# Threshold attention and an MLP mixer on one core: the order of work in the first row, and a weight conversion with one two-operand VectorE step

## The chip, the cores and the metric

The kernel runs on one core of a Trainium2 chip. The metric is the device time of one execution in microseconds (us). Executions of one kernel mostly agree within 0.3%; the state of a run is judged by the clock granted to TensorE and by comparison with the fastest run of the same kernel, and all runs used here are fast ones. Ratios below are the mean time of one kernel's fast runs over that of the other's fast runs of the same rounds, so they are not quite the ratios of the medians that stand beside them.

Engine names in the profile: PE is TensorE (PEld its weight loads), DVE is VectorE, ACT is ScalarE, POOL is GpSimd, SP is SyncE, which here issues DMAs.

## The reference

```python
scores = np.matmul(q, k.transpose(0, 1, 3, 2)) / 8          # q, k, v: 8 x 8 x 576 x 64
thresh = np.max(scores, axis=-1, keepdims=True) - tau
scores = np.where(scores >= thresh, scores, -1e9)
attn = softmax(scores) ; x = heads side by side of attn @ v  # x: 8 x 576 x 512
h   = np.maximum(x^T @ w_tok1, 0) @ w_tok2                   # mixes tokens
u   = x + h^T
out = u + np.maximum(u @ w_ch1, 0) @ w_ch2                   # mixes channels
```

The four weights arrive as 64-bit floats. Before their first use the kernel turns them into 32-bit floats, in 31 pieces, of which 26 have 512 columns.

## The kernel before

The program walks over units: a unit is 128 queries of two heads. For each it makes scores (TensorE), their maxima (VectorE), a bias (GpSimd), a Prelu that applies the threshold and an exponential with sums (ScalarE), and, one unit later, reciprocals (VectorE) and the scaling by them (GpSimd). Two units later the weights of attention are transposed. In the first row (units 0 to 17, batch 0) TensorE does that in three groups of three, each into one PSUM buffer, of which there are two; VectorE or ScalarE then copies the group into SBUF. From the second row on, other code with DMAs does this, and the mixer of the batch before fills TensorE.

```python
def turn(u, third):                     # first row only
    ps = ps_tr.tile([P, MAIN], F32, tag="tr", ...)            # pool of two PSUM buffers
    for c in range(3): nc.tensor.transpose(out=ps[:, c, :], in_=e[...], identity=ident)
    on = nc.scalar.copy if third == 1 and u % 2 else nc.vector.tensor_copy
    on(out=eTs[key][:, 3*third : 3*third+3, ...], in_=ps)

for u in range(...):                    # cut to what the change touches; w = u - 2
    scores(u)                           # TensorE; then maxima on VectorE, bias on GpSimd
    ...                                 # values of earlier units, norm(u - 1)
    if b_now: weight(2)                 # second row: 2 of 6 conversion steps a unit
    else:     weight_to(2.25 * (u - 1.5))
    ...
    for i in range(3): turn(w, i)       # first row
    ...
    if on: weigh(u)                     # Prelus and exponentials, ScalarE
    if b_now: weight(2)
    elif u == 0: ...
    else: weight_to(2.25 * (u - 1))     # the rest of 2.25 steps a unit
```

`weight` runs conversion steps. A piece has three on VectorE, two passes on ScalarE for the piece after it, and an addition on GpSimd, after which the next load into that buffer may start. In the traces VectorE runs its instructions in the order in which the program issues them (in the unit from 43.65 us shown below: maxima, reciprocal, steps, copies). The pool of two buffers decides when the program is built which buffer each group gets; it need not alternate.

Of the kernel before, what the change touches and what calls it, by code (L numbers as in the profile page):

```python
# [9 lines left out]
F32 = mybir.dt.float32  # L10
U32 = mybir.dt.uint32
I32 = mybir.dt.int32
I64 = mybir.dt.int64
AF = mybir.ActivationFunctionType
ALU = mybir.AluOpType
# [6 lines left out]
def kernel(  # L22
# [25 lines left out]
    nc = tc.nc  # L48
# [113 lines left out]



    raws = {}

    def load_piece(i):
# [16 lines left out]
    def wide(i):  # L184
        return i < len(pieces) and pieces[i][1].dtype == I64

    def on_scalar(i, part):
        if wide(i):
            lo, hi, h2 = raws[i]
            if part == 0:  # L190
                nc.scalar.activation(out=lo.bitcast(I32), in_=lo, func=AF.Copy, scale=2.0**-29)
            else:
                nc.scalar.activation(out=h2, in_=hi.bitcast(F32), func=AF.Square)

    def on_vector(i, part):
        if wide(i):
            dst = pieces[i][0]
            lo, hi, h2 = raws[i]
            bits = dst.bitcast(U32)
            if part == 0:  # L200
                nc.vector.tensor_scalar(
                    out=bits, in0=hi, scalar1=3, scalar2=0x3FFFFFFF, op0=ALU.logical_shift_left, op1=ALU.bitwise_and
                )
            elif part == 1:
                nc.vector.scalar_tensor_tensor(  # L205
                    out=bits, in0=hi, scalar=0xC0000000, in1=bits, op0=ALU.bitwise_and, op1=ALU.bitwise_or
                )
            else:
                nc.vector.scalar_tensor_tensor(out=dst, in0=h2, scalar=2.0**-30, in1=dst, op0=ALU.is_ge, op1=ALU.mult)

    def on_gpsimd(i):
        if i >= 0:
# [10 lines left out]
    def weight(n):  # L223

        nonlocal steps_done
        for k in range(steps_done, min(steps_done + n, 3 * len(pieces) + 1)):
            i, part = divmod(k, 3)
            if part == 0:
                on_gpsimd(i - 1)
                if i:  # L230
                    load_piece(i - 1 + NRAW)
            else:
                on_scalar(i + 1, part - 1)
            on_vector(i, part)
            steps_done = k + 1

    def weight_to(x):

        weight(max(int(x) - steps_done, 0))
# [36 lines left out]
    def in_blocks(b):  # L276
        return b > 0
# [10 lines left out]
    def scores(u):  # L288
        b, p0, t = units[u]
        sc = [  # L290
            (ps_3rd if b == 0 and (2 * u + h) % 3 == 2 else ps_sc).tile([P, 2, MAIN], F32, tag="sc", name=f"sc{h}_{u}") for h in range(2)
        ]
        if t == SHARED:
            parts = [(b * NP + p0, slice(MAIN, S), slice(0, 64)), (b * NP + p0 + 1, slice(0, LAST), slice(64, P))]
        else:
            o = P * t if t < SHARED else LAST + P * (t - SHARED - 1)
            parts = [(b * NP + p0 + (t > SHARED), slice(o, o + P), slice(0, P))]
        order = [(f, part, h) for f in range(2) for part in parts for h in range(2)]
        for f, (n, cols, rows), h in order if b else sorted(order, key=lambda o: o[2]):
            r = slice(D * h, D * h + D)  # L300
            qT, kT = heads[n]
            nc.tensor.matmul(sc[h][rows, f, 0:HS], lhsT=qT[r, cols], rhs=kT[r, HS * f : HS * f + HS], start=True, stop=True)  # L302
        mx = small.tile([P, 2], F32, tag="mx", name=f"mx_{u}")
        bias = small.tile([P, 2], F32, tag="bias", name=f"bias_{u}")
        for h in range(2):
            c = slice(h, h + 1)
            nc.vector.tensor_reduce(out=mx[:, c], in_=sc[h][:, :, 0:HS], axis=AX.XY, op=ALU.max)  # L307
            nc.gpsimd.tensor_scalar(out=bias[:, c], in0=mx[:, c], scalar1=toff, scalar2=-SCALE, op0=ALU.add, op1=ALU.mult)  # L308
        st[u] = sc, bias

    def weigh(u):
        sc, bias = st.pop(u)
        rs = small.tile([P, 2], F32, tag="rs", name=f"rs_{u}")
        e = work.tile([P, 2 * S], F32, tag="e", bufs=3, name=f"e_{u}")
        for h in range(2):
            eh = e[:, S * h : S * h + S].rearrange("p (f x) -> p f x", f=2)
            nc.scalar.activation(out=eh, in_=sc[h][:, :, 0:HS], func=AF.Prelu, bias=bias[:, h : h + 1], scale=SCALE, alpha=STEEP)  # L317
        st[u] = e, rs

        if b_now:  # L320
            fill(0.2)
        for h in range(2):
            eh = e[:, S * h : S * h + S]
            nc.scalar.activation(out=eh, in_=eh, func=AF.Exp, bias=ntau, accum_out=rs[:, h : h + 1])  # L324
            if b_now:
                fill(0.2)
# [13 lines left out]
    def turn(u, third):  # L340

        b, p0, t = units[u]
        key, place = (b, p0, t // GU), t % GU
        e = st[u]

        if third == 0 and place == 0:
            eTs[key] = work.tile([P, NK, GU * P], F32, tag="T", name=f"eT_{u}")
        if third == 2:
            st.pop(u)
        ps = ps_tr.tile([P, MAIN], F32, tag="tr", name=f"tr{third}_{u}")[:, 0 : 3 * P].rearrange("p (c x) -> p c x", c=3)  # L350
        for c in range(3):
            k0 = (3 * third + c) * P
            nc.tensor.transpose(out=ps[:, c, :], in_=e[:, k0 : k0 + P], identity=ident)  # L353
        on = nc.scalar.copy if third == 1 and u % 2 else nc.vector.tensor_copy
        on(out=eTs[key][:, 3 * third : 3 * third + 3, P * place : P * place + P], in_=ps)

    def turn_blocks(u):
# [149 lines left out]
    def fill(share):  # L507
        nonlocal credit
        credit += share * quota
        while todo and credit > 0:  # L510
            cost, step = todo.popleft()
            credit -= cost
            step()
        if not todo:
            credit = 0.0
# [18 lines left out]
    b_now = 0  # L534
# [12 lines left out]
    for u in range(len(units) + LAG + 4):  # L547
        on = u < len(units)
        if u == UB:
            late.close()  # L550
            ps_mm = ctx.enter_context(tc.tile_pool(name="ps_mm", bufs=2, space=bass.MemoryType.PSUM))
        if on:
            b_now, p0, t = units[u]
            n = b_now * NP + p0
        w = u - LAG
        back = 0 <= w < len(units)
        if on:
            scores(u)

        last = False  # L560
        if due and not in_blocks(due[0][1]):
            last = values_due(u)
        if 0 < u <= len(units):
            norm(u - 1)
        if b_now:
            weight(2)
        else:

            weight_to(2.25 * (u - 1.5))
        while copies:  # L570
            copies.popleft()()
        if last:
            push(0)
        if back:
            wb, wp, wt = units[w]
            if not in_blocks(wb):
                for i in range(3):
                    turn(w, i)
            if wt % GU == GU - 1:
                g = wt // GU  # L580
                if g < 2:
                    split_middle(wb * NP + wp + g)
                due.append((u + (2 if in_blocks(wb) else 1), wb, wp, g))
        if b_now:
            fill(0.4)
        if back and in_blocks(wb):
            turn_blocks(w)
        if b_now:
            weight(2)
        if on:  # L590
            weigh(u)
        elif b_now:
            fill(0.6)
        if b_now:
            weight(2)
        elif u == 0:
            on_scalar(0, 0)
            on_scalar(0, 1)
        else:
            weight_to(2.25 * (u - 1))  # L600
        if on:


            when = {3: (2, 0, 2), 4: (2, 2, 4), 5: (2, 4, 6), 6: (2, 6, 8), 8: (3, 0, 3), 0: (1, 3, 6), 1: (1, 6, 8)}
            if u == 0:
                load_qk(1, (nc.sync, nc.sync), range(0, 3))
            if t in when:
                m, lo, hi = when[t]
                if n + m < len(pairs):
                    load_qk(n + m, (nc.scalar if b_now else nc.sync,) * 2, range(lo, hi))  # L610
            if t in (3, 7) and n + 2 + t // 4 < len(pairs):
                load_v(n + 2 + t // 4)
            if t == 2:
                prep(n + 1)
            if t == 7 and n + 2 < len(pairs):
                prep(n + 2)
        if due and in_blocks(due[0][1]):
            values_due(u)
# [31 lines left out]
```

## Time and profile before

| | before |
|---|---|
| median, lowest, highest of 3 runs | 1380.67, 1376.87, 1382.66 us |
| span of the profiled run | 1375.1 us |
| TensorE busy | 1322.7 us, 96% |
| VectorE, ScalarE, GpSimd busy | 588.2, 581.8, 356.0 us |

The page's picture of the kernel before, in 40 slices of 34.4 us each (a digit is the busy share in tenths):

```profile
PE   6877799999999999999999999999999999999998
DVE  6788875445444443434244444434333453201000
```

TensorE has room only in the first six slices, about 206 us. From 16 to 206 us VectorE is busy for 156.9 us and TensorE for 155.2; ScalarE (123.3) and GpSimd (110.5) have less to do. The prediction below shows these stages one by one. The profiled run is the fastest of the three (1376.94 us in the record of the profile), so its stages may be shorter than typical; ratios, not two profiles, carry the sizes below.

### The profile page before, as it was taken

What the parts mean: (1) busy time and instruction counts of PE and PEld (TensorE: products, weight loads), DVE (VectorE), ACT (ScalarE), POOL (GpSimd) and SP (SyncE); (2) the same over time, 40 slices, a digit from 0 to 9 for tenths busy, and PEclk for the clock granted to TensorE, in tenths of its full rate; (3) what the DMA queues carried; (4) which work ended last, traced back from release to release, by engine and by line L of the source; (5) the groups of instructions that cost most, each with busy time, mean ns of one, the idle gap of its engine ahead of it and who ended that gap; (6) DMA issues with size and microseconds to landing.
All of it is one profiled execution on the core that took longest, in us unless ns stands there. A gap on an engine that the chain in (4) does not pass through costs nothing.

```text
span 1375.1 us, 17691 instructions
## 1 busy us (share of the span) xinstructions
PE 1322.7 (96%) x6226; PEld 817.9 (59%) x6226; DVE 588.2 (43%) x1017; ACT 581.8 (42%) x1288; POOL 356.0 (26%) x683
## 2 busy tenths in 40 slices
PE   6877799999999999999999999999999999999998
PEld 3444465646565666565665567565656576575675
DVE  6788875445444443434244444434333453201000
ACT  5666654454445444443434444353333444120110
POOL 4555653222222222222122222222121222100000
PEclk9988999999999999999999999999999999999999
DMA  5434655454544354433344435434433442400000
GB/s 121 98 96 125 183 142 124 100 123 98 122 109 114 82 121 94 113 88 95 77 100 94 113 77 123 106 83 98 103 87 75 107 103 63 115 1 16 8 11 21
DMA packets 278871, 128.20 MB, mean 93 GB/s; under 512 B 200896, under 2 KB 271552, under 8 KB 278784
## 3 DMA queue, kind: packets, MB, share of 16 engines
q1 hardware_dynamic: 150176, 111.06, 32.0%
q10 hardware_dynamic: 128608, 16.01, 7.3%
q8 instruction: 50, 0.82, 0.3%
q14 instruction: 37, 0.30, 0.1%
HBM read 43.25 MB, written 9.44 MB: 38 GB/s over the span
## 4 chain that ended last, share of the span: by engine, by line
PE 85%; DVE 7%; DMA 2%; SPq 2%; ACT 1%; issue 1%; POOL 1%; ACTq 0%; DVEq 0%; POOLq 0%
PE c L486 26%; PE c L470 26%; PE sc L302 11%; PE pv L413 9%; PE t L441 5%; PE t L448 3%; PE pv L408 3%; DVE mx L307 2%; SPq L374 2%; PE tx L432 1%; PE c L482 1%; DMA eT<-T 1%; PE tr L353 1%; DVE wc L205 1%; ACT e L317 1%
## 5 line engine op out<-in xcount | busy, mean ns | idle before, releaser
L307 DVE TENSOR_REDUCE mx<-sc 128x1 f32<-128x576 f32 x288 | 204.5, 751 | 487.9 <-PE sc L302 487.5
L470 PE MATMUL c<-xT,wc 128*128 128x256 f32 (+1 forms) x1920 | 399.4, 362 | 2.1 <-DVE xT L452 1.2
L486 PE MATMUL c<-wc,g 128*128 128x512 f32 x864 | 390.5, 597 | 0.0
L470 PEld LDWEIGHTS c<-xT,wc 128*128 128x128 f32 x1920 | 334.5, 191 | 71.5 <-issue 27.6
L308 POOL TENSOR_SCALAR bias<-mx,toff 128x1 f32<-128x1 f32 x288 | 82.8, 288 | 799.3 <-DVE mx L307 742.3
L317 ACT ACTIVATE e<-sc,bias 128x576 f32<-128x576 f32 x288 | 199.6, 739 | 162.0 <-POOL bias L308 161.4
L486 PEld LDWEIGHTS c<-wc,g 128*128 128x128 f32 x864 | 157.8, 190 | 175.7 <-issue 174.0
L471 ACT ACTIVATE g<-c 128x256 f32<-128x256 f32 (+1 forms) x240 | 86.7, 362 | 334.1 <-PE c L470 317.9
L324 ACT ACTIVATE e<-e,ntau 128x576 f32<-128x576 f32 x288 | 220.7, 771 | 0.0
L335 POOL TENSOR_SCALAR e<-e,rr 128x576 f32<-128x576 f32 x288 | 215.6, 761 | 15.8 <-DVE rr L332 4.3
L302 PE MATMUL sc<-kT,qT 64*128 64x288 f32 (+1 forms) x1280 | 196.6, 447 | 11.1 <-DVE kT L284 7.1
L365 DVE STREAM_TRANSPOSE T<-e 128x1152 f32<-128x1152 f32 x126 | 172.1, 1366 | 6.3 <-DMA eT<-T 2.6
L302 PEld LDWEIGHTS sc<-kT,qT 64*128 64x128 f32 (+1 forms) x1280 | 107.4, 184 | 98.3 <-issue 59.1
L413 PE MATMUL pv<-eT,lv 128*64 128x384 f32 (+1 forms) x1024 | 136.8, 409 | 0.0
L413 PEld LDWEIGHTS pv<-eT,lv 128*64 128x64 f32 x1024 | 76.1, 138 | 51.0 <-issue 43.6
L491 DVE COPY o<-c 128x512 f32<-128x512 f32 x36 | 24.9, 692 | 177.5 <-PE c L486 177.5
L418 ACT COPY xT<-pv 128x384 f32<-128x384 f32 (+1 forms) x56 | 21.0, 401 | 157.5 <-PE pv L413 157.5
L448 PE MATMUL t<-w,a 128*128 128x288 f32 x256 | 75.2, 421 | 7.2 <-DVE xT L452 5.3
L441 PE MATMUL t<-x_sb,w 128*128 128x512 f32 x160 | 72.1, 598 | 0.0
L448 PEld LDWEIGHTS t<-w,a 128*128 128x128 f32 x256 | 45.6, 191 | 32.2 <-issue 11.4
L452 DVE TENSOR_TENSOR xT<-xT,t 128x288 f32<-128x288 f32 x64 | 28.2, 446 | 80.5 <-PE t L448 80.0
L324 ACT ACTIVATION_READ_ACCUMULATOR e<-e,ntau 128x1 f32 x288 | 56.5, 196 | 0.0
(44 smaller groups left out, 554.7 us busy)
## 6 DMA issues: line engine op xcount, KB each, us to landing
eT<-T SPq DMA_DIRECT2D x672, 108.0 KB, 2.2
scratch<-in_moe_w_ch_dram SPq DMA_DIRECT2D x24, 512.0 KB, 3.7
lv<-in_v_dram SPq DMA_DIRECT2D x32, 288.0 KB, 3.3
out_dram<-o SPq DMA_DIRECT2D x36, 256.0 KB, 2.2
lk<-in_k_dram ACTq DMA_DIRECT2D x111, 72.0 KB, 2.6
lq<-in_q_dram ACTq DMA_DIRECT2D x106, 72.0 KB, 2.3
lq<-in_q_dram SPq DMA_DIRECT2D x22, 72.0 KB, 3.2
lk<-in_k_dram SPq DMA_DIRECT2D x17, 72.0 KB, 3.3
```

The lines of the kernel that those rows point to most:

```text
L302: nc.tensor.matmul(sc[h][rows, f, 0:HS], lhsT=qT[r, cols], rhs=kT[r, HS * f : HS * f + HS], start=True, stop=True)
L307: nc.vector.tensor_reduce(out=mx[:, c], in_=sc[h][:, :, 0:HS], axis=AX.XY, op=ALU.max)
L317: nc.scalar.activation(out=eh, in_=sc[h][:, :, 0:HS], func=AF.Prelu, bias=bias[:, h : h + 1], scale=SCALE, alpha=STEEP)
L324: nc.scalar.activation(out=eh, in_=eh, func=AF.Exp, bias=ntau, accum_out=rs[:, h : h + 1])
L335: nc.gpsimd.tensor_scalar(out=eh, in0=eh, scalar1=rr[:, h : h + 1], scalar2=1.0, op0=ALU.mult, op1=ALU.mult)
L365: nc.vector.transpose(out=T[:, :, place, :].rearrange("p a (c x) -> p c a x", c=NK), in_=e.rearrange("p (c a x) -> p c a x", c=NK, a=4))
L413: nc.tensor.matmul(to[r], lhsT=lv[:, j, :], rhs=e[j], start=False, stop=(c == NI - 1), skip_group_check=True)
L441: nc.tensor.matmul(ps, lhsT=w1[:, t, P * m : P * m + P], rhs=x_sb[:, t, :], start=(t == 0), stop=(t == NT - 1))
L448: nc.tensor.matmul(ps, lhsT=s["a"][:, m, P * c : P * c + P], rhs=w2[:, m, HS * f : HS * f + HS], start=(m == 0), stop=(m == NTK - 1))
L470: nc.tensor.matmul(ps, lhsT=wc1[:, j, c, :], rhs=uT[:, c, GR * i : GR * i + n], start=(c == 0), stop=(c == NCC - 1))
L471: nc.scalar.activation(out=s["g"][:, j, 0:n], in_=ps, func=AF.Relu)
L486: nc.tensor.matmul(flat, lhsT=s["g"][:, j, P * t : P * t + P], rhs=wc2[:, j, :], start=False, stop=(j == NJ - 1), skip_group_check=True)
```

## The change

It does two things. In the first row, Prelus and exponentials of a unit are issued ahead of the transposes, all conversion steps of the unit are issued there too, and ScalarE copies the middle group of every unit. In the conversion, the weight's absolute value is limited and scaled in one-operand steps, so that one step with two tensor operands remains where there were two.

```diff
@@ on_scalar: second pass
-                nc.scalar.activation(out=h2, in_=hi.bitcast(F32), func=AF.Square)
+                nc.scalar.activation(out=h2, in_=hi.bitcast(F32), func=AF.Abs)
@@ on_vector: three steps
-   (1) tensor_scalar(out=bits, in0=hi, scalar1=3, scalar2=0x3FFFFFFF, logical_shift_left, bitwise_and)
-   (2) scalar_tensor_tensor(out=bits, in0=hi, scalar=0xC0000000, in1=bits, bitwise_and, bitwise_or)
-   (3) scalar_tensor_tensor(out=dst, in0=h2, scalar=2.0**-30, in1=dst, is_ge, mult)
+   (1) tensor_scalar(out=h2, in0=h2, scalar1=2.0**-15, scalar2=2.0**16, max, mult)
+   (2) tensor_scalar(out=bits, in0=h2.bitcast(U32), scalar1=3, scalar2=0, logical_shift_left, bitwise_or)
+   (3) scalar_tensor_tensor(out=bits, in0=hi, scalar=0x80000000, in1=bits, bitwise_and, bitwise_or)
@@ turn
-        on = nc.scalar.copy if third == 1 and u % 2 else nc.vector.tensor_copy
+        on = nc.scalar.copy if third == 1 else nc.vector.tensor_copy
@@ loop over units, first row
-            weight_to(2.25 * (u - 1.5))
+            weight_to(2.25 * (u - 1))
+            if on:
+                weigh(u)
 ...                                    # turns
-        if on:
+        if on and b_now:
             weigh(u)
 ...
-        else:
-            weight_to(2.25 * (u - 1))
```

(The calls in the middle part are shortened; operations and constants are complete.)

More of the change, by code (lines that the diff above doesn't have):

```diff
@@ L200, in on_vector @@
             if part == 0:
+                nc.vector.tensor_scalar(out=h2, in0=h2, scalar1=2.0**-15, scalar2=2.0**16, op0=ALU.max, op1=ALU.mult)
+            elif part == 1:
                 nc.vector.tensor_scalar(
-                    out=bits, in0=hi, scalar1=3, scalar2=0x3FFFFFFF, op0=ALU.logical_shift_left, op1=ALU.bitwise_and
-                )
-            elif part == 1:
-                nc.vector.scalar_tensor_tensor(
-                    out=bits, in0=hi, scalar=0xC0000000, in1=bits, op0=ALU.bitwise_and, op1=ALU.bitwise_or
-                )
-            else:
-                nc.vector.scalar_tensor_tensor(out=dst, in0=h2, scalar=2.0**-30, in1=dst, op0=ALU.is_ge, op1=ALU.mult)
+                    out=bits, in0=h2.bitcast(U32), scalar1=3, scalar2=0, op0=ALU.logical_shift_left, op1=ALU.bitwise_or
+                )
+            else:
+                nc.vector.scalar_tensor_tensor(
+                    out=bits, in0=hi, scalar=0x80000000, in1=bits, op0=ALU.bitwise_and, op1=ALU.bitwise_or
+                )
     def on_gpsimd(i):
```

## The prediction

> **What bounds the kernel now.** I read the page's busy totals first, then the table of stretches over the first 206 us, then TensorE's waits in that stretch, then the chain that ended last, and then VectorE's and GpSimd's instructions in order of time.
>
> TensorE is busy for 1322.7 of 1375.1 us, so at most 52 us of idling are to be had. The stretches show where they lie.
>
> ```profile
> core 0: us, PE busy (x) PEld busy (x) DVE busy (x) ACT busy (x) POOL busy (x), PEclk, DMA share, GB/s
> 16.00:106.00 90.00, 72.76 (x432) 43.85 (x430) 72.84 (x154) 60.10 (x127) 51.37 (x84) 0.91 0.36 85
> 106.00:149.00 43.00, 31.50 (x132) 16.52 (x130) 39.35 (x61) 31.48 (x64) 26.93 (x31) 0.84 0.50 134
> 149.00:206.00 57.00, 50.97 (x249) 34.24 (x249) 44.72 (x69) 31.70 (x68) 32.19 (x38) 0.97 0.66 169
> ```
>
> The reader is to see three stages. From 16 to 106 us runs the first row (units 1 to 17 of batch 0): TensorE and VectorE are both 81% busy, so neither alone is the bound, and they wait for each other in turn. From 106 to 149 us, when six conversion steps fall in each unit, VectorE is busy 39.35 of 43 us (92%): it is the bound, and TensorE idles 11.5 us. From 149 to 206 us TensorE idles 6 us more. A separate cut at 206 us gives TensorE 1159.6 busy of the remaining 1169 us: from there it is the bound. What matters is therefore how much earlier the program arrives at the TensorE-bound part; nothing after it changes.
>
> ```profile
> PE tr L353 <- DVE eT L355: 17.7, 8, 3.6
> PE t L448 <- DVE xT L452: 4.4, 3, 2.2
> PE sc L302 <- ACT e L317: 3.7, 3, 1.9
> PE tr L353 <- ACT eT L355: 3.1, 5, 0.8
> ```
>
> These are TensorE's largest waits from 16 to 206 us (total us, times, longest us). Its third group of transposes waits until VectorE has copied an earlier group out of PSUM, and that copy stands in VectorE's queue behind a unit's maxima and conversion steps. ScalarE's share is only 3.1 + 3.7 us.
>
> ```profile
> 110.86 1.12 DVE L209 SCALAR_TENSOR_TENSOR wc<-h,wc 128x512 f32<-128x512 f32 x1
> 111.90 0.41 DVE L201 TENSOR_SCALAR wc<-scratch 128x512 uint32<-128x512 uint32 x1
> 112.35 1.68 DVE L205 SCALAR_TENSOR_TENSOR wc<-scratch,wc 128x512 uint32<-128x512 uint32 x1
> 114.13 0.69 DVE L209 SCALAR_TENSOR_TENSOR wc<-h,wc 128x512 f32<-128x512 f32 x1
> ...
> 110.15 1.28 POOL L215 TENSOR_TENSOR wc<-wc,scratch 128x512 int32<-128x512 int32 x1
> 112.06 1.42 POOL L215 TENSOR_TENSOR wc<-wc,scratch 128x512 int32<-128x512 int32 x1 [0.63 <-DVE wc L209]
> ```
>
> Here are VectorE's three conversion steps and GpSimd's addition (start us, duration us). Undisturbed, the one-operand step takes 0.41 us and each two-operand step 0.69. The step at 112.35 takes 1.68 and ends just 0.55 us after GpSimd's addition does: it stood still for that addition.
>
> **What the Trainium skill says.** "VectorE: DVE Perf Modes", section "The perf-mode tier table", caps fp32 `tensor_scalar` from SBUF at twice the rate of fp32 `tensor_tensor`, since the second read port is free for it. The trace agrees: from one form with 288 columns to one with 512, the one-operand step grows from 0.29 to 0.41 us (0.54 ns a column), the two-operand step from 0.44 to 0.69 (1.1 ns). "SBUF — State Buffer", section "SBUF: two separate sides", says that VectorE (in a two-port mode or with two SBUF inputs) and GpSimd lock one port pair for a whole instruction. The trace agrees with that too, in the 1.68 us above, and also for the one-operand step, which reaches 1.51 us at its slowest. So a one-operand step is shorter, but it does not escape GpSimd. "ScalarE: Activation LUTs", section "Table sets: the hidden batching unit", has abs in every table set; the trace has one table load (1.28 us). The changed kernel as built has one as well, so Abs instead of Square should cost the same 0.67 us.
>
> **The change, part by part.**
>
> Conversion. Each weight piece had one one-operand and two two-operand steps; now it has two and one. By start-to-start distances undisturbed, these are 0.33 and 0.61 us at 512 columns, 0.20 and 0.36 at 288, so a piece saves 0.28 or 0.16 us. There are 26 pieces of 512 columns, 4 of 288 and one small one: 26 x 0.28 + 4 x 0.16 + 0.1 = 8.0 us of VectorE time. Waits for GpSimd should stay: its additions are the same 31, each released at the same place, and the second step of the next piece, whichever kind, runs into one. They cost VectorE about 0.6 us a step where they occur, which I leave unchanged.
>
> Copies. All 18 middle transposes of the first row are now copied by ScalarE, before only the odd ones: nine copies of 0.47 us, 4.2 us, leave VectorE and come to ScalarE (0.475 us each there). Together VectorE loses 12.2 us of its 157 between 16 and 206 us.
>
> Order in the first row. ScalarE's Prelus and exponentials of a unit now precede the copy of a group of transposes from two units back. Before, ScalarE idled 23.2 us over nine copies waiting for transposes, up to 6.1 us, with ready Prelus behind. The built program confirms one effect: the first-half score matmuls of most units no longer have a wait on ScalarE. Only the 3.7 us above can come of that directly.
>
> Against this, the second call of the pacing is folded into the first. Of 2.25 steps a unit, before about one stood ahead of the copies and the others behind; now all 2.25 do. They then lie on the loop: maxima, steps, first copy, third transposes, next scores, maxima. In addition, in odd units the third transposes used to wait for ScalarE's early copy (0.57 us at a time); in the built program they wait for VectorE's first copy in nearly all units.
>
> One first-row unit without values, 512 columns, worked through: two maxima 1.33, reciprocal 0.27, steps 2.25 x (2 x 0.33 + 0.61) / 3 = 0.95, copy 0.48, third transposes 0.55, first half of the scores 0.6, and some 0.3 for hand-overs: 4.5 us. With 288 columns the steps are 2.25 x 0.25 = 0.57, so 4.1. Before, such units took 3.9 to 5.7 us from maximum to maximum, mean 4.7 over eight of them. Three units in which the 1.4 us of q and k transposes follow take about 1.2 us more than a plain one. Units with values are set by TensorE (scores, values 3.6 to 4.9 us, transposes) and took 4.9 to 8.0, of which I expect 0.3 to 0.5 back. From u = 3 to 17: about ten other units at 0.35 is 3.5 us, five with values at 0.4 is 2, together 5.5.
>
> Second row, units 18 to 23, to about 163 us: VectorE-bound, two pieces a unit, 2 x 0.28 = 0.56 us a unit, six units, 3.4 us; the copies of units 16 and 17 add 0.5.
>
> From there to 206 us TensorE idles 5 us, in waits for values' blocks by DMA, for VectorE's sums and for ScalarE behind a late weight load. VectorE is 78% busy there. Four more units with two pieces could give 2.2; I take 1.
>
> Sum: 5.5 + 3.9 + 1 = 10.4 us. 1380.67 - 10.4 = 1370.3; I say 1370.
>
> **Rivals.**
>
> First: VectorE's queue order cancels the gain in the first row. All steps ahead of the first copy put 1.25 steps, 0.5 us, on the loop of each of 15 units, and the lost early ScalarE copy adds to it in odd units. For it: transposes waiting for VectorE are already the largest wait, 17.7 us. Against it: VectorE is 81% busy there, and often has no idle time before its maxima, so order matters less than the sum. The first row would then gain nothing or lose 3 us: 1376 to 1379.
>
> Second: ScalarE becomes the bound of the first row. A unit then has Prelus 1.3, exponentials with their reads 1.7, a copy 0.45, and 1.5 conversion passes of 0.56, 0.84: 4.3 us, about the loop above. Its conversion passes stand ahead of the next Prelus, and the first transposes of the next unit wait for its copy. For it: 4.3 against 4.1 to 4.5 leaves no slack. Against it: 60.1 of 90 us busy now, and the value units have slack. It would limit the row's gain to some 3 us: 1373.
>
> Third: more is gained, because TensorE is slowed by its own pauses. "TensorE: Matmul & The Clock Gate", Part 1, describes half the clock after some 3.4 us of idling. The trace shows a granted 0.84 between 106 and 149 us, and eight score matmuls at 2.3 us there against 1.24 at full clock. If shorter pauses keep the clock up, half-clock score groups return about 1 us each; some five of them bring 1365.
>
> Fourth: the second row is set by weight loads and block transfers through SyncE's queue, where 16 issues last 10 to 12 us, so VectorE's gain after 149 us is hidden. I have mostly allowed for it.
>
> **Range and chances.** If the first and second rivals hold together and half the second row's gain is hidden, 1378; with the clock's help and all of VectorE's 12.2 us on the path, 1361. I give 1361 to 1378. Faster by 2% needs 27 us, over half of all idling by TensorE, which neither part can reach: 0.03. Slower by 2% would need a new wait of 1.5 us in every unit of both rows, and the program order holds none: 0.01. The rest, 0.96, is within 2%.
>
> **What would show it.** Right: of the two new one-operand steps of a 512-column piece the undisturbed duration is 0.41 us each, the two-operand one 0.69; VectorE's busy total falls from 588 to about 576, ScalarE's rises by 4; the last conversion step, now at 197.96 us, moves 9 to 10 us earlier, of which 5 to 6 are there by unit 18's maxima (now at 106.2); TensorE's busy time after that is the same. ScalarE's 23.2 us of waiting ahead of copies nearly vanishes. Wrong: transposes wait over 20 us for VectorE's copies (first rival); ScalarE is over 80% busy in the first row (second); granted clock near 1 before 149 us (third); or the first one-operand step takes 0.69 us, so that in-place fp32 maximum and product get no double rate, which would take 8 us from VectorE's saving.

## The result

The changed kernel took 1386.62 us (median of 6 runs, 1385.39 to 1389.01), the kernel before 1381.87 in the same rounds (1376.87 to 1382.66). The ratio is 1.0042, 95% interval 1.0025 to 1.0058: slower by some 5.8 us. The forecast of 1370 and its range of 1361 to 1378 were both missed, on the other side of the kernel before. Within 2% it is the same, which had been given 0.96.

The busy totals of the changed kernel, and the three stretches that the prediction showed of the kernel before (columns: us, then busy time and count of PE, PEld, DVE, ACT, POOL, then granted clock, DMA share, GB/s):

```profile
PE 1326.8 (96%) x6226; PEld 817.3 (59%) x6226; DVE 573.4 (41%) x1008; ACT 587.4 (42%) x1297; POOL 357.3 (26%) x683
```

```profile
16.00:106.00 90.00, 65.93 (x364) 37.49 (x362) 57.91 (x131) 59.91 (x126) 48.12 (x76) 0.92 0.33 75
106.00:149.00 43.00, 35.41 (x170) 19.60 (x170) 33.95 (x61) 27.40 (x54) 24.98 (x32) 0.80 0.46 120
149.00:206.00 57.00, 49.21 (x245) 33.55 (x244) 45.59 (x77) 35.12 (x73) 34.15 (x41) 0.94 0.65 178
```

The granted clock of 0.92 in the first line is too high. The trace's first record of the clock is at 38.88 us in the changed kernel (at 24.05 us in the one before), and what lies ahead of it counts as 1.00. But TensorE was slow there: three transposes took 0.90 us and eight score matmuls 2.30, where later ones take 0.55 and 1.25.

```profile
23.16:38.88 15.72, 12.19 (x52) 6.45 (x54) 10.23 (x23) 9.95 (x21) 8.98 (x15) 1.00 0.28 58
```

```profile
32.64 0.90 PE L354 MATMUL tr<-ident,e 128*128 128x128 f32 x3 [1.83 <-DVE eT L356]
33.48 2.30 PE L303 MATMUL sc<-kT,qT 64*128 64x288 f32 x8
```

VectorE lost its work as planned (588.2 to 573.4 us busy in all), but in the first 90 us both it and TensorE got less done: VectorE is busy 57.91 instead of 72.84 us, TensorE 65.93 instead of 72.76. They wait more for each other. TensorE's waits from 16 to 206 us in the changed kernel name the place:

```profile
PE tr L354 <- DVE eT L356: 28.8, 12, 4.7
PE sc L303 <- ACT e L318: 3.5, 3, 1.9
PE t L449 <- DVE xT L453: 2.6, 2, 2.2
...
PE tr L354 <- ACT eT L356: 0.8, 2, 0.6
```

Transposes waited 17.7 us for VectorE's copies before, now 28.8, although VectorE has fewer copies to make; the waits for ScalarE's copies, 3.1 us before, are 0.8.

I measure two rows by the starts of the maxima. The first row runs from those of unit 3 to those of unit 18: 22.85 to 106.18 us before (83.3 us), 23.16 to 116.83 after (93.7 us). The second runs from unit 18 to unit 29: 99.9 us before, 98.5 after. The conversion ends within the second row, and from there TensorE is 99% busy in both. So the first row lost 10.3 us in this pair of profiles, the second gained 1.4.

### The loop, in one unit

VectorE and TensorE in the changed kernel, unit 6 to 7, in order of time (start us, duration us, instructions; in brackets the idle time before and what ended it):

```profile
43.65 1.42 DVE L308 TENSOR_REDUCE mx<-sc 128x1 f32<-128x576 f32 x2 [0.68 <-PE sc L303]
44.99 0.16 DVE L332 TENSOR_SCALAR rr<-rs 128x2 f32<-128x2 f32 x1
45.18 0.17 DVE L333 RECIPROCAL rr<-rr 128x2 f32<-128x2 f32 x1
45.26 0.29 DVE L202 TENSOR_SCALAR h<-h 128x288 f32<-128x288 f32 x1
45.59 0.32 DVE L204 TENSOR_SCALAR w<-h 128x288 uint32<-128x288 uint32 x1
45.83 0.54 DVE L356 COPY eT<-tr 128x384 f32<-128x384 f32 x1
47.01 0.56 DVE L356 COPY eT<-tr 128x384 f32<-128x384 f32 x1 [0.64 <-PE tr L354]
48.24 0.76 DVE L308 TENSOR_REDUCE mx<-sc 128x1 f32<-128x576 f32 x1 [0.68 <-PE sc L303]
```

```profile
46.43 0.55 PE L354 MATMUL tr<-ident,e 128*128 128x128 f32 x3 [2.07 <-DVE eT L356]
46.90 1.25 PE L303 MATMUL sc<-kT,qT 64*128 64x288 f32 x8
```

The reader is to see a closed ring. From start to start: maxima 1.34, reciprocal 0.27, two conversion steps 0.57, first copy until the third transposes start 0.60, third transposes 0.47, scores until the next maxima start 1.34; the sum is 4.59 us, exactly the distance between the maxima. Nothing in it overlaps. TensorE idles 2.07 us of it, and VectorE 1.3.

The kernel before, unit 15 to 16, on VectorE, TensorE and ScalarE:

```profile
89.17 1.42 DVE L307 TENSOR_REDUCE mx<-sc 128x1 f32<-128x576 f32 x2
90.51 0.16 DVE L331 TENSOR_SCALAR rr<-rs 128x2 f32<-128x2 f32 x1
90.70 0.17 DVE L332 RECIPROCAL rr<-rr 128x2 f32<-128x2 f32 x1
90.78 0.67 DVE L209 SCALAR_TENSOR_TENSOR wc<-h,wc 128x512 f32<-128x512 f32 x1
91.37 1.02 DVE L355 COPY eT<-tr 128x384 f32<-128x384 f32 x2
92.30 0.92 DVE L201 TENSOR_SCALAR wc<-scratch 128x512 uint32<-128x512 uint32 x1
93.14 0.74 DVE L307 TENSOR_REDUCE mx<-sc 128x1 f32<-128x576 f32 x1
```

```profile
90.45 0.55 PE L353 MATMUL tr<-ident,e 128*128 128x128 f32 x3 [0.57 <-ACT eT L355]
90.92 1.43 PE L302 MATMUL sc<-kT,qT 64*128 64x288 f32 x8
```

```profile
89.92 0.48 ACT L355 COPY eT<-tr 128x384 f32<-128x384 f32 x1 [2.17 <-PE tr L353]
```

Here the third transposes were given the buffer that ScalarE empties at 90.40. They start at 90.45, while VectorE is still at its maxima; its own first copy comes at 91.37. Scores of the next unit are ready before VectorE wants them, and it has no idle time at all, with two 512-column steps in 3.97 us. This happened in five of the units whose groups ScalarE copied (units 3, 7, 9, 13 and 15). In the changed kernel as built, no such unit is left in the first row: the pool, when building, gives every third group the buffer behind VectorE's first copy, and ScalarE's copy, now behind the Prelus and exponentials, comes late (in unit 6 at 47.79 us, after the third transposes at 46.43).

### The profile page after: what moved, and what is told of

Same layout as the page of the kernel before. It is cut to its first block, busy times and chain, and to the rows that moved or that the text cites. A ratio compares the mean times of both kernels' runs of the same rounds, so it can differ in the third digit from the quotient of the medians.

```text
span 1384.3 us, 17694 instructions
## 1 busy us (share of the span) xinstructions
PE 1326.8 (96%) x6226; PEld 817.3 (59%) x6226; DVE 573.4 (41%) x1008; ACT 587.4 (42%) x1297; POOL 357.3 (26%) x683
## 4 chain that ended last, share of the span: by engine, by line
PE 87%; DVE 7%; DMA 2%; ACT 1%; issue 1%; SPq 1%; POOL 0%; ACTq 0%; DVEq 0%; POOLq 0%
PE c L487 26%; PE c L471 26%; PE sc L303 12%; PE pv L414 9%; PE t L442 5%; PE t L449 4%; PE pv L409 3%; DVE mx L308 3%; PE tx L433 1%; PE c L483 1%; PE tr L354 1%; SPq L375 1%; DVE h L202 1%; ACT e L318 1%; DVE wc L208 1%
## 5 line engine op out<-in xcount | busy, mean ns | idle before, releaser
L336 POOL TENSOR_SCALAR e<-e,rr 128x576 f32<-128x576 f32 x288 | 218.7, 772 | 15.2 <-DVE rr L333 4.3
L354 PE MATMUL tr<-ident,e 128*128 128x128 f32 x162 | 31.2, 327 | 30.9 <-DVE eT L356 28.8
```

The lines of the kernel that those rows point to most:

```text
L336: nc.gpsimd.tensor_scalar(out=eh, in0=eh, scalar1=rr[:, h : h + 1], scalar2=1.0, op0=ALU.mult, op1=ALU.mult)
```

## The experiments

Theory A: the order is to blame. Every unit now closes the ring through VectorE's queue, and the conversion steps, all ahead of the copies, lie on it. Theory B: the conversion is to blame, through new collisions or its new wait for ScalarE. Theories C to F are side questions named where they come. All runs were correct and timed in five rounds beside the kernel before.

| run | conversion | Prelus | steps | ScalarE copies | ratio (95% interval) | median us | first row us | second row us | half clock us |
|---|---|---|---|---|---|---|---|---|---|
| before | old | behind | in two | odd | 1 | see text | 83.3 | 99.9 | 18.3 |
| changed | new | ahead | all ahead | all | 1.0042 (1.0025 to 1.0058) | 1386.62 | 93.7 | 98.5 | 32.8 |
| e1 | new | behind | in two | odd | 0.9969 (0.9952 to 0.9986) | 1375.61 | 85.1 | 97.8 | 17.1 |
| e2 | old | ahead | all ahead | all | 1.0073 (1.0054 to 1.0092) | 1390.16 | 94.8 | 100.4 | 27.3 |
| e3 | new | ahead | all behind | all | 0.9976 (0.9957 to 0.9996) | 1375.76 | 84.4 | 97.9 | 17.1 |
| e4 | old | behind | in two | all | 0.9964 (0.9944 to 0.9983) | 1374.28 | 80.4 | 99.7 | 5.3 |
| e5 | old | ahead | in two | odd | 1.0041 (1.0027 to 1.0055) | 1386.33 | 89.4 | 100.2 | 25.1 |
| e6 | new | ahead | in two | all | 0.9993 (0.9980 to 1.0007) | 1379.05 | 85.6 | 98.4 | 24.8 |
| e7 | new | behind | in two | all | 0.9944 (0.9928 to 0.9960) | 1372.15 | 77.7 | 100.8 | 2.6 |
| e8 | new | behind | all behind | all | 0.9995 (0.9981 to 1.0009) | 1380.02 | 83.9 | 98.8 | 16.3 |
| e9 | e7, third group in ScalarE's buffer | | | | 0.9961 (0.9946 to 0.9975) | 1374.65 | 81.5 | 101.4 | 6.4 |
| e10 | e7, third group in VectorE's buffer | | | | 1.0000 (0.9988 to 1.0011) | 1380.48 | 87.6 | 98.9 | 22.8 |
| e11 | e8, third group in ScalarE's buffer | | | | 0.9995 (0.9984 to 1.0007) | 1378.76 | 86.5 | 98.4 | 15.2 |
| e12 | e7, Abs pass first | | | | 0.9959 (0.9946 to 0.9973) | 1374.25 | 78.2 | 97.7 | 3.1 |

The medians of the kernel before were 1379.3 to 1380.63 in these rounds. Rows are from one profile each and can vary by a few us between executions: unit 14 took 8.5, 6.9 and 9.2 us in e4, e7 and e9, the last two with the same instructions. The ratios have 5 to 14 runs. The last column is the part of the first row in which TensorE had half its clock by the trace's clock records, with the time ahead of a trace's first record counted as half.

**e1: the new conversion alone.** Only the hunks `on_scalar` and `on_vector` of the diff.

> The new conversion alone, with the order, the pacing in two calls and the ScalarE copies of the kernel before. Theory A (the loss comes from the order: every unit of the first row now closes a loop maxima, reciprocal, steps, first copy, third transposes, scores, maxima): this part is harmless and saves VectorE time, first row (maxima of unit 3 to maxima of unit 18) 80 to 83 us against 83.3 before and 93.7 in the changed kernel, ratio to the kernel before 0.996 to 0.999. Theory B (the conversion is to blame: its first step now waits for ScalarE's Abs, or its one-operand steps collide more with GpSimd): first row over 86 us, ratio 1.002 to 1.006.

Measured 0.9969, as theory A had it. The first row of its profile, 85.1 us, is 2 us longer than that range, the second is 2.0 us shorter than before. Theory B as the cause of the loss falls: the conversion is worth about 4.3 us of 1379.

**e2: the new order alone.** The rest of the diff with the old conversion.

> The new order of the first row (Prelus ahead, pacing folded into one call, all middle copies on ScalarE) with the old conversion. Theory A: the loop is as in the changed kernel with steps that are 0.09 us longer on average, so first row 94 to 98 us, ratio 1.005 to 1.009, with over 24 us of transposes waiting for VectorE's copies. Theory B: first row 80 to 85 us, ratio 0.997 to 1.001.

Measured 1.0073, first row 94.8 us, with 33.0 us of transposes waiting for VectorE's copies from 16 to 206 us. The two parts multiply: 0.9969 x 1.0073 = 1.0042, the ratio of the whole change. So the order costs some 10 us and the conversion returns some 4.

**e3: steps behind the copies.**

```diff
-            weight_to(2.25 * (u - 1))          # ahead of the turns
+        else: weight_to(2.25 * (u - 1))        # at the end of the unit
```

> The changed kernel with all conversion steps of the first row behind the copies of the transposes in VectorE's queue; Prelus still ahead, all middle copies still on ScalarE. Theory A: the steps term (0.7 to 1.4 us a unit) leaves the loop, VectorE does it while TensorE makes scores: first row 80 to 85 us, ratio 0.995 to 0.999. Theory C (the loss comes from the buffers alone, since the third transposes wait for VectorE's first copy in every unit, wherever the steps stand): first row over 88 us, ratio 1.001 to 1.004.

Measured 0.9976. With Prelus ahead and with VectorE's buffer in nearly every unit, taking the steps off the ring is enough to undo the loss, though transposes still waited 22.5 us for VectorE's copies from 16 to 206 us (28.8 in the changed kernel). Theory C, the buffers alone, falls in that form.

**e4: all middle copies on ScalarE, nothing else.**

```diff
-        on = nc.scalar.copy if third == 1 and u % 2 else nc.vector.tensor_copy
+        on = nc.scalar.copy if third == 1 else nc.vector.tensor_copy
```

> The kernel before with only the copies changed: all 18 middle transposes of the first row by ScalarE, Prelus behind as before, old conversion. As built, the third transposes wait for ScalarE in 12 of 18 units, not for VectorE. Theory A: those units take tr and scores off the loop through VectorE's queue, as odd units did before; first row 76 to 82 us, ratio 0.994 to 0.999. If ScalarE is made the bound by nine more copies that wait for transposes ahead of Prelus, first row 84 to 88 us, ratio 1.000 to 1.004.

Measured 0.9964, first row 80.4 us. One line of the change alone is a gain. In the pool's plan the third group then waits for ScalarE in 12 of 18 units (12 waits, 12.2 us, from 16 to 110 us), and the granted clock over the first row was 0.97 against 0.90 before.

**e5: Prelus ahead, nothing else.**

```diff
+            if on: weigh(u)                    # ahead of the turns
 ...
-        if on: weigh(u)
+        if on and b_now: weigh(u)
```

> The kernel before with only the Prelus and exponentials put ahead of the turns in the first row; pacing in two calls, copies of odd units on ScalarE, old conversion. As built, the third transposes then wait for VectorE's first copy in all units, where before five odd ones (units 1, 5, 7, 11, 13) took ScalarE's buffer. Theory A: the loop runs through VectorE in every unit with one step on it: first row 86 to 92 us against 83.3, ratio 1.002 to 1.006. Theory D (putting Prelus ahead is good as meant, and only the folded pacing costs): first row 79 to 83 us, ratio 0.995 to 0.999.

Measured 1.0041. Putting Prelus ahead is harmful by itself, about 5.7 us; theory D falls. ScalarE's waiting ahead of its copies, which the change set out to remove, fell in the changed kernel from 23.2 to 7.2 us as expected, but it moved rather than vanished: ScalarE's waiting for GpSimd's biases, ahead of its Prelus, rose from 7.5 to 27.4 us (16 to 206 us).

**e6: the changed kernel with pacing in two.**

```diff
-            weight_to(2.25 * (u - 1))
+            weight_to(2.25 * (u - 1.5))
 ...
+        else: weight_to(2.25 * (u - 1))
```

> The changed kernel with the pacing in two calls again (one step ahead of the copies, the rest behind); all else as changed. Theory A: 1.25 steps of 0.42 us and some waits for GpSimd leave the loop of 15 units, 6 to 9 us: first row 84 to 88 us against 93.7, ratio 0.998 to 1.001, between the changed kernel (1.0042) and the one with all steps behind (0.9976). Theory C (buffers alone): first row over 91 us, ratio over 1.002.

Measured 0.9993. Against the changed kernel's 1.0042 that is 0.5%, near 7 us, for moving about 1.25 steps a unit behind the copies. So both halves of the new order cost: the Prelus' place, and the steps' place.

**e7: new conversion and all middle copies, in the old order.** The hunks of e1 and e4 together.

> New conversion and all middle copies on ScalarE, in the old order (Prelus behind, pacing in two calls). As built the third transposes wait for ScalarE in 12 of 18 units. Theory A: the gains of the two parts add, since one lies in the first row (80.4 us with the copies alone) and one in the second (1.4 to 2 us): first row 79 to 83 us, ratio 0.992 to 0.996. If they do not add, since the first row is then bound by ScalarE or TensorE: ratio 0.996 to 0.998.

Measured 0.9944, median 1372.15 us, with 1380.63 for the kernel before in the same rounds. The parts add (0.9969 x 0.9964 = 0.9933). This is the lowest ratio found; it beats both kernels.

**e8: e7 with all steps behind the copies.** The edit of e3 on e7.

> As the run before, with all steps of the first row behind the copies. Theory A: where the third transposes still wait for VectorE (6 to 9 units as built), one step of 0.4 us leaves the loop, but the pool hands out the buffers differently and fewer units wait for ScalarE: first row 78 to 84 us, ratio 0.991 to 0.997, not clearly apart from the run before.

Measured 0.9995, a clear miss: moving the step that e7 has ahead of the copies behind them took e7's gain away. (e3 is no counterpart, since it moved all 2.25 steps; the like move with Prelus ahead, from e6 to e3, gave 0.9993 and 0.9976, with intervals that overlap.) e11 below looks for the reason.

**e9 and e10: the buffer by itself.** Both are e7 with the pool's choice fixed. Instruction by instruction, the order on all five engines was compared and is the same as in e7; only the PSUM buffers differ. (The cut leaves out two places where other tiles of the same pool, those of values and of the mixer's transposes, also go through tr_tile.)

```diff
+    def tr_tile(name, same=False):
+        nonlocal tr_at
+        tr_at = tr_at if same else 1 - tr_at
+        return ps_tr.tile([P, MAIN], F32, tag=f"tr{tr_at}", bufs=1, name=name)
-        ps = ps_tr.tile([P, MAIN], F32, tag="tr", name=f"tr{third}_{u}")
+        ps = tr_tile(name=f"tr{third}_{u}", same=third == 2)   # e9; e10: without same
```

> The run with new conversion and ScalarE copies in the old order (e7: first row 77.7 us, ratio 0.9944) with one thing changed: the PSUM buffer of the third transposes is fixed to the one that ScalarE has just emptied, in all 18 units (e7: 12 of 18). The order of instructions on every engine is the same. Theory A (who empties that buffer decides): first row 75 to 78 us, ratio 0.992 to 0.996; little more than e7, since the remaining units are those with values, where VectorE waits for TensorE anyway.

> The same with the opposite choice: the third transposes always take the buffer of the first, which VectorE empties behind maxima and a step. The order of instructions on every engine is that of e7 and of the run before. Theory A: the loop through VectorE closes in every unit as in the changed kernel, with one step on it: first row 84 to 90 us, ratio 1.000 to 1.005, transposes wait over 20 us for VectorE's copies. Theory E (the order of the instructions decides, the buffer does not): first row 77 to 79 us, ratio 0.994 to 0.996.

TensorE's waits for group buffers from 16 to 110 us, e9 and then e10:

```profile
PE tr L359 <- ACT eT L361: 14.6, 17, 1.6
...
PE tr L359 <- DVE xT L426: 2.7, 5, 1.9
```

```profile
PE tr L359 <- DVE eT L361: 17.8, 11, 2.2
PE tr L359 <- DVE xT L426: 1.2, 5, 0.3
```

e9 measured 0.9961 and e10 1.0000, on the same chip, with intervals apart: 0.4%, about 5.4 us, for a choice of buffer alone. Theory E, the order of instructions decides and the buffer does not, falls. e10's row, 87.6 us, lies in my range; its waits at 17.8 us fell short of the 20 I expected. e9's row was above its range (81.5 us, with 9.2 in unit 14) and e9 is no better than e7, so forcing ScalarE's buffer where the pool had not chosen it brought nothing.

**e11: e8 with ScalarE's buffer.**

> Buffers as in e9, all steps behind the copies as in e8 (first row 83.9 us, ratio 0.9995, a miss of mine). If e8 lost because the pool handed fewer units ScalarE's buffer, fixing the buffers brings it to 75 to 79 us, ratio 0.992 to 0.996. If it lost because three steps in a row stand ahead of the next maxima, it stays at 81 to 85 us, ratio 0.997 to 1.001.

Measured 0.9995 again, with a row of 86.5 us, above both ranges: the buffer is not why e8 lost. The profiles offer two reasons. VectorE's first step, now ahead of the next unit's transposes and maxima, waits for ScalarE's Abs: from 16 us to the end of the row 5.6 us in e11 and 6.2 in e8, against 0.3 in e7 (from 16 us to the end of the second row 13.3, 14.8 and 8.5). And TensorE had half its clock for 15.2 us of the row in e11 and 16.3 in e8, against 2.6 in e7; in unit 5 of e11 (10.4 us) 16 value matmuls took 5.01 us, in unit 11 2.75. Neither reason was tested by itself.

**The second row, and e12.** The new conversion also made a new wait. VectorE's first step used to read the loaded weight; now it reads the result of ScalarE's second pass. VectorE's wait for it, changed kernel from 16 to 215 us, and what the first step waited for in the kernel before from 16 to 206 us:

```profile
DVE h L202 <- ACT h L194: 7.1, 4, 3.9
```

```profile
DVE wc L201 <- DMA scratch<-in_moe_w_ch_dram: 1.8, 2, 1.5
```

The largest one, on ScalarE and then on VectorE of the changed kernel:

```profile
203.86 0.68 ACT L192 ACTIVATE scratch<-scratch 128x512 int32<-128x512 uint32 x1 [4.75 <-DMA scratch<-in_moe_w_ch_dram]
...
204.44 0.67 ACT L194 ACTIVATE h<-scratch 128x512 f32<-128x512 f32 x1
```

```profile
205.15 0.43 DVE L202 TENSOR_SCALAR h<-h 128x512 f32<-128x512 f32 x1 [3.90 <-ACT h L194]
```

A late weight load holds ScalarE for 4.75 us, and VectorE stands behind two passes of it. e12 exchanges the passes:

```diff
             if part == 0:
-                (low words: Copy, scale 2**-29)
+                (Abs of the high words into h2)
             else:
-                (Abs of the high words into h2)
+                (low words: Copy, scale 2**-29)
```

> As e7 (new conversion, all middle copies on ScalarE, old order; ratio 0.9944) with ScalarE's two conversion passes of a piece exchanged: Abs first, then the low words. Theory F (the missing part of the second row's gain is VectorE's new wait for ScalarE's Abs, 7.1 us in the changed kernel and 8.5 in e7, where it waited 1.8 us for loads before): the wait falls by about one pass, 0.6 us, for each of its five or so occurrences, to 5 to 6.5 us; second row (maxima of unit 18 to maxima of unit 29) 98 to 100.5 us against 100.8 in e7; ratio 0.992 to 0.995. If the wait is only the shadow of late weight loads or of TensorE, the row stays at 100.5 to 101.5 us and the ratio at 0.994 to 0.996.

VectorE's wait fell from 8.5 us in e7 to 4.4, more than expected:

```profile
DVE h L201 <- ACT h L191: 4.4, 2, 3.5
```

The second row was 97.7 us in its profile against 100.8. But the ratio, 0.9959, is not below e7's 0.9944; the two ran on different chips and their intervals overlap. The ratio lies in the range that I gave for the other case, in which the wait is only a shadow. A gain from the exchange is not shown.

## Why the prediction was wrong

**The failing step is the first row's unit, worked through, and the rival set aside because of it.** The prediction had the ring in its list, in the right order, and added it up to 4.1 us with 288-column steps and 4.5 with 512. It measured 4.59 in unit 6, without values, at full clock and with two 288-column steps. The term that was wrong is "first half of the scores 0.6": the maxima start 1.34 us after the scores do, only when all eight score matmuls are through, since those of the two heads run side by side (in the trace's single records they start in pairs, 0.01 to 0.02 us apart). The other terms were near: maxima 1.34 for 1.33, reciprocal 0.27, steps 0.57 for 0.57, first copy 0.60 for 0.48, transposes 0.47 for 0.55; the 0.3 for hand-overs was already inside them. That the steps agree is luck: I had 2.25 of 0.25 us, and two took 0.33 and 0.24. My sum had 0.20 and 0.33 us for a one-operand step of 288 and of 512 columns; a step that reads its result starts 0.32 and 0.44 us after it in the traces. Units with three steps were longer still: between 60.80 and 66.24 us the third step, one with two operands, took 0.80 us instead of 0.44, and the unit 5.44 us.

**The comparison with before was the larger fault.** I took the mean of 4.7 us before as if the same ring had closed then. It had not in five units, where ScalarE handed over the buffer early and scores were made under VectorE's work; the unit from 89.17 us shows it. The prediction names this loss ("in the built program they wait for VectorE's first copy in nearly all units") but gives it no number. The five units took 23.2 us before and 28.4 us in the changed kernel, 5.2 of the 10.3 us lost.

**The first rival was right in mechanism and too small.** I put it at 0 to 3 us of loss in the first row, arguing from VectorE's 81% that "order matters less than the sum". Its sign, transposes waiting over 20 us for VectorE's copies, came true with 28.8. e2 puts the order at 1.0073, near 10 us, of which e5 gives the Prelus' place about 5.7 and the step from e6 to the changed kernel gives the folded pacing near 7, with the copies taking some back (e4: about 5). These come from runs on different bases and need not add up to 10. A share of 81% on two engines that hand work to each other does not mean that either is the bound.

**VectorE's saving was right.** Undisturbed one-operand steps of 512 columns, the uint32 shift as well as the fp32 maximum and product, took 0.41 us and two-operand ones 0.69; the busy total fell by 14.8 us (12.2 predicted) and ScalarE's rose by 5.6 (4 predicted). TensorE's busy time behind the second row is the same, 1159.58 and 1159.65 us from unit 29 to the end.

**The second row gave 1.4 us, not 4.9.** The last conversion step, expected 9 to 10 us ahead of 197.96, came at 207.25 us. The term of 0.56 us a unit is right where VectorE is the bound: units 25 and 26 took 17.27 to 17.28 us together in every run with the old conversion and 16.07 to 16.09 in every run with the new, 0.6 a unit. Units 18 and 19 gave 1.35 us. But from unit 20 to 25 it gave nothing (50.8 and 50.9 us), and units 27 and 28 took 1.1 us longer. What I left out is the wait for Abs. Its total is measured; how much of the missing gain is due to it is not, since e12 halved it without a shown gain in time. That part stays open. (TensorE's idling before the change from 163 to 206 us, 5 us in the prediction, is 3.4 by the profile.)

**The other rivals.** ScalarE did not become the bound (59.9 of 90 us). The clock, the third rival, works here too, but against the change. TensorE had half its clock for 18.3 us of the first row before and for 32.8 in the changed kernel, and was busy for 17.1 and 29.1 us of that. If that work takes half as long at full clock, as the durations above suggest, up to 6 us of the 10.3 lie in the slower clock (my estimate from these four numbers). Units 3 and 4, which in the changed kernel lie ahead of 38.88 us, lost 3.8 us of the 10.3. Over all runs, those with over 22 us at half clock have rows of 85.6 to 94.8 us, those with under 7 us rows of 77.7 to 81.5; e9 and e10 differ by 16.4 us. The slower clock followed on waits of TensorE (changed kernel, columns as in the result):

```profile
42.29:45.70 3.41, 2.07 (x15) 1.35 (x14) 2.54 (x7) 1.31 (x4) 0.80 (x3) 1.00 0.46 111
66.19:69.60 3.41, 1.34 (x11) 0.94 (x11) 2.66 (x7) 2.12 (x4) 2.11 (x4) 1.00 0.97 219
69.60:73.01 3.41, 3.41 (x14) 1.60 (x16) 1.75 (x3) 1.84 (x7) 1.19 (x3) 0.50 0.36 103
```

The reader is to see that after 3.41 us with TensorE busy for 1.34 the clock was 0.50; after 3.41 us with 2.07 it stayed. That the order of work causes the loss is shown by the experiments; how the loss divides between the waits and the slower clock that went with them was not separated, in e4, e7, e9 and e10 neither. The fourth, transfers through SyncE's queue, was not tested.

## What to carry to other kernels

Where two engines hand work to each other and both are some 80% busy, write down the ring for one unit, from start to start, out of one timeline, and look for the units in which it is not closed; a mean over units hides them. Read TensorE's clock off the durations of equal matmuls too, since a trace may show 1.00 until its first clock record. A wait that seems to cost nothing, such as ScalarE's 23 us ahead of its copies here, can be what lets another engine run on, so removing it needs a look at who takes over that buffer. After any reordering, list for each reused buffer who empties it last, since a pool may choose anew, and test parts of a joined change apart: one line of this one (e4) and its conversion (e1) gain 0.6% together, and its order loses 0.7%.

## What the Trainium skill lacked or had wrong

- "TensorE: Matmul & The Clock Gate", Part 1, has the clock fall after an idle window of some 3.4 us. The length of the window fits: the clock of the changed kernel changes at 52.53, 55.95, 69.60 and 73.01 us. But the window need not be idle: from 66.19 to 69.60 us TensorE was busy for 1.34 of 3.41 us, and half the clock followed. Nor does the length of one pause tell: a pause of 2.07 us before 69.02 us was followed by a score group of 2.24 us, another of 2.07 us before 46.43 us by one of 1.25.
- No page that I read treats what the choice between two PSUM buffers is worth when different engines empty them: 5.4 us of 1380 at an identical order of instructions (e9 against e10), waits and clock together.
